# Decode attention on one core: TensorE's loop staggered by one head, K and V loads interleaved, the last head's first V half loaded into a K buffer

## The chip, the cores and the metric

The kernel runs on one core of a Trainium2 chip. The metric is the device time of one execution in microseconds (us). Before the change the median of 14 runs is 650.09 us, the lowest 648.61, the highest 654.18.

A core has engines that run side by side, each with its own instruction stream: PE (TensorE, matrix products), DVE (VectorE), ACT (ScalarE), POOL (GpSimd) and SP (SyncE, which issues loads here). They order themselves by semaphores. Data come from HBM by 16 transfer (DMA) engines, which work through the loads in the order in which SP issues them.

## The reference

```python
B, Hq, Hkv, Sq, Sk, D = 1, 32, 8, 1, 65536, 128     # bfloat16
k = jnp.repeat(k, 4, axis=1); v = jnp.repeat(v, 4, axis=1)
scores = jnp.einsum("bhqd,bhkd->bhqk", q, k) * D ** -0.5
p = softmax(scores)
out = jnp.einsum("bhqk,bhkd->bhqd", p, v)
```

One query row for each of 32 heads; four query heads share one of 8 K/V heads, each with 65,536 keys of 128 numbers. K and V together are 268.4 MB, which are read once; the output is 8 KB. "Head" below means one of the 8 K/V heads with its four queries.

## The kernel before

**Halves and slots.** A head's K, and its V, is loaded in two halves (`load`, L124), each 128 partitions x 256 keys x 128 numbers, 8.4 MB. The text writes K10 for head 1, half 0. The buffer `io` (L73) has three slots of one half each: slot 0 takes every V half, slot 1 the K halves 0, slot 2 the K halves 1. A load may be issued only when its slot has been used. SP issues all loads in one written order (L156 to 162): K00, K01, and then V00, K10, V01, K11, V10, K20 and so on. Ahead of each load SP waits for a count: for a K half that the scores from the slot's last content are done (`s_sc`, L130), for a V half that the slot's values are done (`s_vc`, L136). While SP waits, everything behind it in its order waits too. The last V half (L146 to 154) comes in six pieces, the first issued when the first half of the slot is free (`s_va`).

**A head on the engines.** DVE turns each K half in four quarters of 64 keys, in place (`transposes`, L214), and tells PE by `s_kt`. PE computes scores (L329 to 346): a loop of 8 steps, two steps to a bank of the PSUM tile `sc`, 16 matmuls to a step, 128 in all. The addresses of the matmuls are computed from the loop's counter in registers (`r_k`, `r_w`, `r_o`, L330 to 332). DVE takes the maximum of each bank (`bank_max`), the maxima go across the partitions by way of PE and DVE (`softmax`, L227; PE L347 to 353), and ACT computes the exponentials and their sums (L241). DVE turns the exponentials to weights for the values (`weights`, L249, one V half at a time into the tile `et`), and PE multiplies them with V (`wide`, L357): 64 matmuls for a half, which go in turn to four groups of PSUM rows of `vacc` (`32 * c`). For the last V half four of them are left out, and 16 small matmuls (L392 to 398) take their place, as soon as the last two pieces have landed. DVE adds up the four groups (`collect`, L260), PE adds across partitions (L389), DVE scales (`finish`, L273), and the result is stored.

**PE's order.** PE's program is a loop over the 8 heads (L320). In one turn: clear `sc` and `vacc` with five matmuls, all scores of head h, maximum and row sums of head h, values of head h from V half 0 and half 1, sum across partitions. So no score of head h + 1 is computed before the last value of head h. `take` (L306) is a wait on a semaphore that also takes the count off.

**Around it.** q is loaded four times into four groups of 32 partitions by ACT's queue (L165); DVE turns it (L178), and POOL copies each head's part into `wz` (L208), the moving window of score weights.

Of the kernel before, what the change touches and what calls it, by code (L numbers as in the profile page):

```python
# [21 lines left out]
TAIL = 16  # L22

# [23 lines left out]
def kernel(  # L47
# [29 lines left out]
    q_in = sb("q_in", [P, D], bf16)  # L77
# [23 lines left out]
    pl, fin = pf[0:H, 256:260], pf[0:H, 0:D]  # L101

    s_q, s_ka, s_kb, s_st = sem("s_q"), sem("s_ka"), sem("s_kb"), sem("s_st")
    s_v = [sem(f"s_v{i}") for i in range(4)]
    s_last = sem("s_last")
# [6 lines left out]
    s_sc, s_pe, s_va, s_vb, s_vc = sem("s_sc"), sem("s_pe"), sem("s_va"), sem("s_vb"), sem("s_vc")  # L112
# [16 lines left out]
    def load_k(g, b):  # L129
        SP.wait((s_sc, 8 * (g - 1) + 4 * b + 4 if g else 0))  # L130
        load(k, g, b, 1 + b, (s_ka, s_kb)[b])

    def load_v(g, b):
        n = 2 * g + b
        if g < G - 1:
            SP.wait((s_vc, n))  # L136
            load(v, g, b, 0, s_v[0])
            for s in s_v[1:]:
                sp.sem_inc(s, 16)
        elif b == 0:  # L140
            SP.wait((s_vc, n))
            load(v, g, b, 0, s_v[0], 0, 128)
            load(v, g, b, 0, s_v[1], 128, SL)
            for s in s_v[2:]:
                sp.sem_inc(s, 16)
        else:  # L146
            SP.wait((s_va, n))
            load(v, g, b, 0, s_v[0], 0, 128)
            SP.wait((s_vc, n))
            load(v, g, b, 0, s_v[1], 128, 192)  # L150
            load(v, g, b, 0, s_v[2], 192, 224)
            load(v, g, b, 0, s_v[3], 224, 240)
            load(v, g, b, 0, s_last, 240, 248)
            load(v, g, b, 0, s_last, 248, 256)
# [3 lines left out]
    for g in range(G):  # L158
        for b in range(2):
            load_v(g, b)  # L160
            if g < G - 1:
                load_k(g + 1, b)


    for a in range(4):  # L165
        act.dma_start(out=q_in[32 * a:32 * a + 32, :], in_=q[0, :, 0, :]).then_inc(s_q, 16)
# [10 lines left out]
    DV.wait((s_q, 64))  # L177
    d_qT = DV.mark(dve.transpose(  # L178
        out=qT[:, :, :].rearrange("p s n -> p (s n)"), in_=q_in[:, :].bitcast(u32)
    ))  # L180
# [9 lines left out]
    d_sel = DV.mark(dve.tensor_reduce(  # L190
        out=sely[:, :], in_=selq[:, :].rearrange("p (y h) -> p y h", h=H), axis=AX.X, op=ALU.add
    ))

# [5 lines left out]
    for g in range(G):  # L199
        if g == 0:  # L200
            GP.wait((s_dv, d_qT))
            GP.after(p_ident)
        else:
            GP.wait((s_sc, 8 * g))
        for a in range(4):
            r = slice(32 * a, 32 * a + 32)
            c0 = 28 + 32 * a
            gp.tensor_copy(  # L208
                out=wz[r, :, c0:c0 + H].rearrange("p (s w) h -> p s w h", s=2),
                in_=qTb[r, :, :, g, :],  # L210
            ).then_inc(s_w, 1)


    def transposes(g, b):  # L214
        DV.wait(((s_ka, s_kb)[b], 16 * (g + 1)))
        for t0 in range(0, SL, PS):
            part = io[:, (1 + b) * SL + t0:(1 + b) * SL + t0 + PS, :].rearrange("p t d -> p (t d)")
            dve.transpose(out=part.bitcast(u32), in_=part.bitcast(u32)).then_inc(s_kt, 1)  # L218
            yield

    def bank_max(g, b):
        DV.wait((s_sc, 8 * g + 2 * b + 2))
        return DV.mark(dve.tensor_reduce(  # L223
            out=mx[:, b:b + 1], in_=sc[:, 512 * b:512 * b + 512], axis=AX.X, op=ALU.max
        ))

    def softmax(g):  # L227
        dve.tensor_reduce(out=mg[:, :], in_=mx[:, :], axis=AX.X, op=ALU.max).then_inc(s_mg, 1)
        DV.wait((s_pe, 4 * g + 1))
        n = DV.mark(dve.tensor_reduce(  # L230
            out=m4[:, :], in_=pt[0:1, 0:P].rearrange("o (x h) -> o h x", h=H), axis=AX.X, op=ALU.max
        ))
        DV.after(n)
        dve.tensor_scalar_mul(
            out=nrow[:, :, :], in0=m4[:, None, :].to_broadcast([1, 32, H]), scalar1=-SCALE
        ).then_inc(s_nr, 1)
        DV.wait((s_pe, 4 * g + 2))
        d_nmb = DV.mark(dve.tensor_copy(out=nmb[:, :], in_=pb[:, 0:1]))  # L238
        ACTQ.wait((s_dv, d_nmb))
        for b in range(4):  # L240
            a = act.activation(  # L241
                out=ex[:, b, :], in_=sc[:, 512 * b:512 * b + 512], func=ACT.Exp, bias=nmb[:, :],
                scale=SCALE, accum_out=ls[:, b:b + 1],
            )
            ACTQ.mark(a)
        act.wait_ge(s_ac, ACTQ.n)
        act.sem_inc(s_ls, 1)
# [6 lines left out]
    def reciprocal(g):  # L254
        DV.wait((s_pe, 4 * g + 3))
# [25 lines left out]
    d_rl = None  # L281
    for g in range(G):
        for _ in transposes(g, 0):
            pass
        if g:
            DV.wait((s_vc, 2 * g))
            collect()
            finish(g - 1, 4 * g, d_rl)
        bank_max(g, 0)
        for i, _ in enumerate(transposes(g, 1)):  # L290
            if i == 1:
                bank_max(g, 1)
        bank_max(g, 2)
        DV.after(bank_max(g, 3))
        softmax(g)
        weights(g, 0)
        d_rl = reciprocal(g)
        DV.wait((s_vc, 2 * g + 1))
        weights(g, 1)
    DV.wait((s_vb, 2 * G))  # L300
    collect()
    finish(G - 1, 4 * G + 1, d_rl)
# [15 lines left out]
    pe.wait_ge(s_gp, p_ident)  # L318
    pe.wait_ge(s_dv, d_sel)
    with nc.Fori(0, G, 1, engines=OrderedEngineSet([PE]), head_slot={PE: 0}) as h:  # L320
# [7 lines left out]
        take(s_w, 4)  # L328
        with pe.Fori(0, 8) as p:  # L329
            r_k = pe.snap(p * (PS * D) + SL * D)  # L330
            r_w = pe.snap((p % 2) * (-16) + 28)
            r_o = pe.snap((p // 2) * 512)
            take(s_kt, 1)
            i = None
            for u in range(4):
                for s in range(2):
                    for e in range(2):
                        i = pe.matmul(  # L338
                            out=bass.AP(sc, r_o, [[2048, P], [1, 512]]),
                            lhsT=bass.AP(wz, r_w + ((2 * s + e) * WB - 4 * u), [[4 * WB, P], [1, P]]),  # L340
                            rhs=bass.AP(
                                io, r_k + (u * D + 64 * s + e), [[IO, P], [4 * D, 16], [2, 32]]
                            ),
                            start=False, stop=False, skip_group_check=True,
                        )
            i.then_inc(s_sc, 1)
        take(s_mg, 1)  # L347
        pe.transpose(out=pt[0:1, 0:P], in_=mg[:, :], identity=ident[:, :]).then_inc(s_pe, 1)  # L348
        take(s_nr, 1)
        pe.matmul(  # L350
            out=pb[:, 0:1], lhsT=nrow[:, :, :].rearrange("o x h -> o (x h)"), rhs=one[:, :],
            start=True, stop=True,
        ).then_inc(s_pe, 1)
        take(s_ls, 1)
        pe.matmul(out=pl, lhsT=sel[:, :], rhs=ls[:, :], start=True, stop=True).then_inc(s_pe, 1)  # L355

        def wide(ch, tt):  # L357
            c = tt % 4
            return pe.matmul(  # L359
                out=vacc[32 * c:32 * c + 16, :, :],  # L360
                lhsT=et[:, ch // 2, tt * 32 + 16 * (ch % 2):tt * 32 + 16 * (ch % 2) + 16],
                rhs=io[:, PS * ch + 4 * tt:PS * ch + 4 * tt + 4, :],
                start=False, stop=False, skip_group_check=True,
            )

        with pe.Fori(0, 2) as j:
            take(s_et, 2)
            take(s_v[0], 16)
            for tt in range(16):
                wide(0, tt)  # L370
            for tt in range(16):
                i = wide(1, tt)
            i.then_inc(s_va, 1)
            take(s_v[1], 16)
            for tt in range(16):
                wide(2, tt)
            take(s_v[2], 16)
            for tt in range(8):
                wide(3, tt)
            take(s_v[3], 16)  # L380
            for tt in range(8, 12):
                i = wide(3, tt)
            i.then_inc(s_vb, 1)
            with pe.If(h * 2 + j < 2 * G - 1):
                for tt in range(12, 16):
                    i = wide(3, tt)
                i.then_inc(s_vc, 1)
        take(s_vs, 1)
        pe.matmul(out=fin, lhsT=sel[:, :], rhs=vs[:, :], start=True, stop=False,  # L389
                  skip_group_check=True).then_inc(s_pe, 1)  # L390
    pe.wait_ge(s_last, 32)
    for x in range(TAIL):  # L392
        t = SL - TAIL + x
        o_ = (12 + x // 4) * 32 + 16 + 4 * (x % 4)
        i = pe.matmul(  # L395
            out=fin, lhsT=et[:, 1, o_:o_ + H], rhs=io[:, t, :], start=False,
            stop=(x == TAIL - 1), skip_group_check=True,
        )
    i.then_inc(s_pe, 1)
# [30 lines left out]
```

## Time and profile before

| | |
|---|---|
| median of 14 runs | 650.09 us |
| the profiled execution | 648.25 us |
| its span, first to last instruction | 646.3 us |
| mean granted PE clock | 0.804 |
| busy: PE, DVE, ACT, POOL | 347.5, 344.2, 23.5, 7.8 us |
| read from HBM | 268.47 MB, 415 GB/s over the span |
| K quarters turned by DVE (L218) | 64 x 4415 ns |
| score matmuls (L338) | 1024, 232.6 us busy |
| value matmuls (L359) | 1020, 92.2 us busy |

All durations come from one profiled execution. Its own time is 1.95 us more than its span, and it lies 1.84 us below the median. The page of the profile cuts the span in 40 slices of 16.2 us; a digit is the busy share in tenths. Groups of instructions are listed with their line, engine, what they write and read, their count, the busy time and the mean duration of one. PE's time has three parts: matmuls (PE), weight loads (PEld) and the sequencer (PEq or PEldq), which reads the program, computes addresses in registers, branches and waits; the sequencer's instructions are not counted as busy. A matmul's recorded duration (0.38 us for 512 columns at full clock) overlaps with its neighbours', so the pace is read from their starts. A number in brackets at the end of a line in order of time is how long the engine had been idle before it, and what ended that.

### The profile page before, as it was taken

To read this page: it belongs to the slowest core of one execution; us is meant where nothing else is said; L and a number is where in the kernel's file an instruction comes from. 1 tells how busy PE (TensorE), PEld (TensorE's weight loads), DVE (VectorE), ACT (ScalarE), POOL (GpSimd) and SP (SyncE) were. 2 spreads that over 40 slices of the span, in tenths; PEclk is the share of its full clock that TensorE was granted. 3 is DMA by queue.
4 is the path that set the end of the run, shared out by engine and by line. 5 is a ranking of instruction groups with operands and counts; after the bars stand their busy time and mean duration, and the time that the engine had idled before them with its cause. 6 is when DMAs were issued, how large, how long until landed. Compare 5 with 4: busy or idle time off the path is not lost. (4 is left out here: it accounts for less than half of the span.)

```text
span 646.3 us, 6464 instructions
## 1 busy us (share of the span) xinstructions
PE 347.5 (54%) x2156; PEld 141.9 (22%) x2156; DVE 344.2 (53%) x221; ACT 23.5 (4%) x65; POOL 7.8 (1%) x40
## 2 busy tenths in 40 slices
PE   0197405973079640876138760498406873088535
PEld 0033102431024210332013320143102331033212
DVE  0498282572917647194552927438292573917501
ACT  0000100001000100001000010000100001000100
POOL 1000000000000000000000000000000000000000
PEclk9999757996569965998759976589757997589975
DMA  9999999999999999999999999999999999999365
GB/s 391 452 393 450 450 398 442 442 414 439 434 426 442 438 418 442 438 418 446 430 426 446 438 414 446 434 418 450 430 422 446 426 434 438 426 435 416 152 286 233
DMA packets 5733, 268.53 MB, mean 416 GB/s; under 512 B 864, under 2 KB 864, under 8 KB 1248
## 3 DMA queue, kind: packets, MB, share of 16 engines
q1 hardware_dynamic: 5480, 268.44, 96.4%
q10 hardware_dynamic: 248, 0.04, 0.0%
q14 instruction: 4, 0.03, 0.0%
q8 instruction: 1, 0.02, 0.0%
HBM read 268.47 MB, written 0.01 MB: 415 GB/s over the span
## 5 line engine op out<-in xcount | busy, mean ns | idle before, releaser
L218 DVE STREAM_TRANSPOSE io<-io 128x4096 uint32<-128x4096 uint32 x64 | 279.5, 4415 | 36.2 <-DMA io<-in_k_dram 36.2
L338 PE MATMUL sc<-io,wz 128*128 x1024 | 232.6, 382 | 31.1 <-PEq L309 31.1
L359 PE MATMUL vacc<-io,et 128*16 128x512 bf16 x1020 | 92.2, 538 | 183.2 <-PEq L309 183.2
L338 PEld LDWEIGHTS sc<-io,wz 128*128 x1024 | 99.1, 97 | 164.6 <-issue 53.2
L359 PEld LDWEIGHTS vacc<-io,et 128*16 128x16 bf16 x1020 | 32.6, 117 | 239.7 <-issue 232.7
L223 DVE TENSOR_REDUCE mx<-sc 128x1 f32<-128x512 f32 x32 | 21.5, 670 | 88.8 <-PE sc L338 88.8
L252 DVE STREAM_TRANSPOSE et<-ex 128x512 bf16<-128x512 bf16 x32 | 21.5, 701 | 52.0 <-PE vacc L359 45.2
L241 ACT ACTIVATE ex<-sc,nmb 128x512 bf16<-128x512 f32 x32 | 21.5, 685 | 587.1 <-DVE nmb L238 587.1
L261 DVE TENSOR_SCALAR vs<-vacc,sely 128x128 f32<-128x128 f32 x8 | 2.8, 351 | 72.7 <-PE vacc L359 72.7
L324 PE MATMUL sc<-zero 128*128 128x512 bf16 x32 | 10.2, 450 | 27.9 <-DVE sely L190 27.1
L355 PE MATMUL pf<-ls,sel 128*4 128x4 f32 x16 | 1.5, 166 | 25.6 <-PEq L309 25.6
L178 DVE STREAM_TRANSPOSE qT<-q_in 128x64 uint32<-128x64 uint32 x1 | 0.2, 246 | 24.3 <-DMA q_in<-in_q_dram 24.3
L208 POOL COPY wz<-qT 32x16 bf16<-32x16 bf16 x32 | 6.1, 190 | 523.0 <-PE sc L338 498.6
L389 PE MATMUL pf<-vs,sel 128*4 128x128 f32 x16 | 3.2, 285 | 13.7 <-PEq L309 13.7
L324 PEld LDWEIGHTS sc<-zero 128*128 128x128 bf16 x32 | 2.8, 103 | 32.2 <-issue 30.7
L264 DVE SCALAR_TENSOR_TENSOR vs<-vacc,sely,vs 128x128 f32<-128x128 f32 x24 | 8.4, 351 | 0.9
L348 PE MATMUL pt<-ident,mg 128*1 128x128 f32 x8 | 2.2, 270 | 8.5 <-PEq L309 8.5
L355 PEld LDWEIGHTS pf<-ls,sel 128*4 128x4 f32 x16 | 0.9, 82 | 26.1 <-issue 26.1
L241 ACT ACTIVATION_READ_ACCUMULATOR ex<-sc,nmb 128x1 f32 x32 | 6.5, 203 | 0.0
L276 DVE TENSOR_SCALAR o<-pf,rl 4x128 bf16<-4x128 f32 x8 | 2.7, 339 | 6.8 <-PE pf L389 4.3
L350 PE MATMUL pb<-one,nrow 1*128 1x1 f32 x16 | 2.8, 241 | 5.7 <-PEq L309 5.7
L256 DVE TENSOR_REDUCE l<-pf 4x1 f32<-4x4 f32 x8 | 1.2, 150 | 8.1 <-PE pf L355 8.1
(25 smaller groups left out, 24.2 us busy)
## 6 DMA issues: line engine op xcount, KB each, us to landing
io<-in_v_dram SPq DMA_DIRECT2D x3, 4096.0 KB, 23.3
io<-in_v_dram SPq DMA_DIRECT2D x1, 2048.0 KB, 14.8
io<-in_v_dram SPq DMA_DIRECT2D x1, 1024.0 KB, 16.9
io<-in_v_dram SPq DMA_DIRECT2D x1, 512.0 KB, 17.7
io<-in_v_dram SPq DMA_DIRECT2D x2, 256.0 KB, 18.0
io<-in_k_dram SPq DMA_DIRECT2D x16, 38.8
io<-in_v_dram SPq DMA_DIRECT2D x14, 28.4
out_dram<-o ACTq DMA_DIRECT2D x7, 1.0 KB
```

Of the source, the lines that this page charges most:

```text
L208: gp.tensor_copy(out=wz[r, :, c0:c0 + H].rearrange("p (s w) h -> p s w h", s=2), in_=qTb[r, :, :, g, :],).then_inc(s_w, 1)
L218: dve.transpose(out=part.bitcast(u32), in_=part.bitcast(u32)).then_inc(s_kt, 1)
L223: return DV.mark(dve.tensor_reduce(out=mx[:, b:b + 1], in_=sc[:, 512 * b:512 * b + 512], axis=AX.X, op=ALU.max))
L241: a = act.activation(out=ex[:, b, :], in_=sc[:, 512 * b:512 * b + 512], func=ACT.Exp, bias=nmb[:, :], scale=SCALE, accum_out=ls[:, b:b + 1],)
L252: dve.transpose(out=et[:, i, :], in_=ex[:, 2 * b + i, :]).then_inc(s_et, 1)
L261: n = DV.mark(dve.tensor_scalar_mul(out=vs[:, :], in0=vacc[:, 0, :], scalar1=sely[:, 0:1]))
L264: i = dve.scalar_tensor_tensor(out=vs[:, :], in0=vacc[:, y, :], scalar=sely[:, y:y + 1], in1=vs[:, :], op0=ALU.mult, op1=ALU.add,)
L324: pe.matmul(out=bank, lhsT=zero[:, 0:P], rhs=zero[:, :], start=True, stop=False, skip_group_check=True,)
L338: i = pe.matmul(out=bass.AP(sc, r_o, [[2048, P], [1, 512]]), lhsT=bass.AP(wz, r_w + ((2 * s + e) * WB - 4 * u), [[4 * WB, P], [1, P]]), rh ...
L350: pe.matmul(out=pb[:, 0:1], lhsT=nrow[:, :, :].rearrange("o x h -> o (x h)"), rhs=one[:, :], start=True, stop=True,).then_inc(s_pe, 1)
L359: return pe.matmul(out=vacc[32 * c:32 * c + 16, :, :], lhsT=et[:, ch // 2, tt * 32 + 16 * (ch % 2):tt * 32 + 16 * (ch % 2) + 16], rhs=io[: ...
L389: pe.matmul(out=fin, lhsT=sel[:, :], rhs=vs[:, :], start=True, stop=False, skip_group_check=True).then_inc(s_pe, 1)
```

## The change

**Loads.** The order becomes K00, K01, V00, K10, K11, V01 and from there K20, V10, K21, V11, ..., K70, V60, K71, V61, V70, V71. K waits on the same condition (its counts are doubled, as a score step now has 8 matmuls); V waits for the values of the V half before it, as it did. V70, the first V half of the last head, goes to slot 1, a K slot, in two parts of 128 keys each, when the scores of K70 are done. V71 goes to slot 0 in six pieces, all issued when the values of V61 are done. q is loaded once, and DVE turns it four times.

**PE.** The loop has 9 turns. In turn h, for j = 0 and 1: scores of half j of head h (if h < 8), then values of half j of head h - 1 (if h > 0). Behind both come maximum and its broadcast for head h. The sum across partitions (`gather`) and the row sums of the head before stand at the beginning of a turn, ahead of the clearing; in the first turn they run on zeros that DVE has written. Score steps have 8 matmuls instead of 16, in a loop inside the loop over j, with both counters in the addresses. V70's values are 16 steps of 4 matmuls with addresses in registers, all into the rows 0 to 15 of `vacc`. The 16 small matmuls now come ahead of the last sum across partitions.

**DVE.** In turn g: turn K half 0 of head g; weights of half 1 of head g - 1; turn K half 1; maxima; reciprocal and `collect` of head g - 1; `softmax` and weights of half 0 of head g; `finish` of head g - 1.

The diff, cut to its core:

```diff
-pl, fin = pf[0:H, 256:260], pf[0:H, 0:D]
+pl, fin = pb[0:H, 8:12], pf[0:H, 0:D]
...
     def load_k(g, b):
-        SP.wait((s_sc, 8 * (g - 1) + 4 * b + 4 if g else 0))
+        SP.wait((s_sc, 16 * g - 8 + 8 * b if g else 0))
...
         elif b == 0:
-            SP.wait((s_vc, n))
-            load(v, g, b, 0, s_v[0], 0, 128)
-            load(v, g, b, 0, s_v[1], 128, SL)
...
+            SP.wait((s_sc, 16 * g + 8))
+            for i in range(2):
+                load(v, g, b, 1, s_u[i], 128 * i, 128 * i + 128)
         else:
-            SP.wait((s_va, n))
-            load(v, g, b, 0, s_v[0], 0, 128)
-            SP.wait((s_vc, n))
...
+            SP.wait((s_vc, 2 * g))
+            for lo, hi, s in zip(CUTS, CUTS[1:], s_v):
+                load(v, g, b, 0, s, lo, hi)
...
-    for g in range(G):
-        for b in range(2):
-            load_v(g, b)
-            if g < G - 1:
-                load_k(g + 1, b)
-    for a in range(4):
-        act.dma_start(out=q_in[32 * a:32 * a + 32, :], in_=q[0, :, 0, :]).then_inc(s_q, 16)
+    load_v(0, 0)
+    load_k(1, 0)
+    load_k(1, 1)
+    load_v(0, 1)
+    for g in range(2, G):
+        for b in range(2):
+            load_k(g, b)
+            load_v(g - 1, b)
+    load_v(G - 1, 0)
+    load_v(G - 1, 1)
+    act.dma_start(out=q_in[:, :], in_=q[0, :, 0, :]).then_inc(s_q, 16)
...
+    GP.wait((s_sc, 16 * G))
+    gp.sem_inc(s_w, 4)
+    for i in range(2):
+        GP.wait((s_u[i], 16))
+        gp.sem_inc(s_un, 128 // UN)
...
+    with nc.Fori(0, G + 1, 1, engines=OrderedEngineSet([PE]), head_slot={PE: 0}) as h:
+        take(s_w, 4)
+        take(s_vs, 1)
+        gather(start=True, stop=True).then_inc(s_pe, 1)
+        take(s_ls, 1)
+        pe.matmul(out=pl, lhsT=sel[:, :], rhs=ls[:, :], start=True, stop=True).then_inc(s_pe, 1)
...
+        with pe.Fori(0, 2) as j:
+            with pe.If(h < G):
+                with pe.Fori(0, 8) as n:
+                    r_k = j * (SL * D) + (n // 2) * (PS * D) + (n % 2) * (2 * D) + SL * D
+                    r_w = (n % 4) * (-8) + 28
+                    r_o = j * 1024 + (n // 4) * 512
+                    take(s_kt, 1)
+                    for u in range(2):
...
+                    i.then_inc(s_sc, 1)
+            with pe.If(h * 2 + j > 1):
+                take(s_et, 2)
+                with pe.If(h * 2 + j == 2 * G):
+                    with pe.Fori(0, SL // UN) as n:
+                        r_v = n * (UN * D) + SL * D
+                        r_e = (n // 8) * 512 + (n // 4) % 2 * 16 + (n % 4) * 128
+                        take(s_un, 1)
+                        for c in range(4):
+                            i = pe.matmul(
+                                out=vacc[0:16, :, :],
+                                lhsT=bass.AP(et, r_e + c * 32, [[1024, P], [1, 16]]),
+                                rhs=bass.AP(io, r_v + c * (4 * D), [[IO, P], [1, 4 * D]]),
+                                start=False, stop=False, skip_group_check=True,
+                            )
+                        i.then_inc(s_vu, 1)
+                with pe.Else():
...
+                    i.then_inc(s_vb, 1)
+                    with pe.If(h < G):
...
+                        i.then_inc(s_vc, 1)
+        with pe.If(h < G):
+            take(s_mg, 1)
...
     for x in range(TAIL):
...
+        if x % 8 == 0:
+            pe.wait_ge(s_v[len(CUTS) - 3 + x // 8], 16)
...
+    pe.wait_ge(s_vs, 1)
+    gather(start=False, stop=True).then_inc(s_pe, 1)
```

Here `UN` is 16, `SL` 256, `G` 8, and `CUTS` is 0, 128, 192, 224, 240, 248, 256.

## The prediction

> **What bounds the kernel now.** I read the 40 slices first, then the stretches at the end, then the order of time around the loads.
>
> ```profile
> DMA  9999999999999999999999999999999999999365
> GB/s 391 452 393 450 450 398 442 442 414 439 434 426 442 438 418 442 438 418 446 430 426 446 438 414 446 434 418 450 430 422 446 426 434 438 426 435 416 152 286 233
> ```
>
> The transfer engines are full in 37 of 40 slices; neither PE (54%) nor DVE (53%) is. So the time is 32 loads of 8.4 MB, plus the stretches in which no load may start. The next view gives stretches of 3 to 4 us; its last two columns are DMA share and GB/s, the one before is the granted PE clock.
>
> ```profile
> 600.00:604.00 4.00, 3.65 (x16) 1.53 (x16) 4.00 (x2) 0.00 (x0) 0.00 (x0) 1.00 0.82 352
> 604.00:608.00 4.00, 3.46 (x16) 1.54 (x16) 0.49 (x1) 0.00 (x0) 0.00 (x0) 1.00 0.00 0
> ...
> 612.00:616.00 4.00, 1.89 (x22) 0.75 (x26) 1.30 (x4) 1.60 (x6) 0.00 (x0) 0.50 0.00 0
> 616.00:619.00 3.00, 3.00 (x40) 1.16 (x36) 0.00 (x0) 0.00 (x0) 0.00 (x0) 0.59 0.23 66
> ```
>
> From about 604.8 to 618.9 nothing moves: 14.1 us. All of K is in, the one V slot still holds the first V half of head 7, and PE does not reach it until the softmax of head 7 is done. That is what the change goes for.
>
> The pace of the loads is read from DVE's waits for K, in order of time:
>
> ```profile
> 82.41 17.43 DVE L218 STREAM_TRANSPOSE io<-io 128x4096 uint32<-128x4096 uint32 x4 [3.31 <-DMA io<-in_k_dram]
> ...
> 585.89 8.77 DVE L218 STREAM_TRANSPOSE io<-io 128x4096 uint32<-128x4096 uint32 x2 [2.52 <-DMA io<-in_k_dram]
> ```
>
> K of head 1, half 0 (call it K10) is load 4, K71 is load 30: (585.89 - 82.41) / 26 = **19.37 us a load**. A load that finds the queue empty costs more:
>
> ```profile
> 617.93 4.40 SPq L125 DMA_DIRECT2D io<-in_v_dram  x6
> ...
> 630.07 3.59 PE L359 MATMUL vacc<-io,et 128*16 128x512 bf16 x32 [10.12 <-PEq L309]
> ```
>
> Half a load took 12.1 us from issue to use, 2.4 more than 19.37 / 2.
>
> **The change, part by part.**
>
> *Order of loads: the gap at 604.8 goes, another comes early.* The new order is K00 K01 V00 K10 K11 V01 K20 V10 K21 V11 and so on. V01 waits until PE has used V00, and PE now uses V00 only behind the scores of K10. V00 lands at 63, K10 at 82.4, K11 at 101.8; SP stands at V01's wait, with K20 and all later loads behind it. So the question is when the scores of K10 end. DVE needs 4.4 us for the first quarter, so PE starts at 86.8. PE's pace then comes from its sequencer. These are the sequencer's rows of one score step of 16 matmuls, and of the loop's edge before it (count, then ns min/median/max):
>
> ```profile
> L338 PEldq FUSED_REGOPS  x17: 74/74/110, 114.0 to 116.7; - x17
> ...
> L338 PEldq ALU_OP  x1: 36/36/36, 114.4 to 114.4; - x1
> ```
>
> ```profile
> L329 PEldq ALU_OP  x1: 32/32/32, 113.4 to 113.4; - x1
> L329 PEldq COMPARE_BRANCH  x1: 209/209/209, 113.5 to 113.5; - x1
> L329 PEldq MOVE  x1: 29/29/29, 113.8 to 113.8; - x1
> ```
>
> Every matmul with a register in its address has one fused register instruction, and in the trace their starts lie 0.153 us apart. The edge, from the ALU_OP at 113.40 to the first fused instruction at 114.05, is 0.64 us. The first matmul's addresses (two heavier fused instructions and one ALU_OP) take 0.45. So a step of 16 is 0.64 + 0.45 + 15 x 0.153 = 3.39 us, just under the 16 x 0.216 = 3.46 of its matmuls: today PE hides it. The change halves the step to 8 matmuls and puts two loop counters into the addresses: about 21 register operations instead of 13 for the first one, which I price at 0.66. A step is then 0.64 + 0.66 + 7 x 0.153 = **2.37 us against 1.73 of matmuls: the sequencer becomes the bound**. Eight steps are 19.0 us a half (14.1 now; DVE's four transposes take 17.4). From 86.8 the first step needs 1.9 without its edge, seven more 16.6, the last matmul 0.4, PE's cold start about 0.8: scores end at 106.4. Two branches and four takes of semaphores (1.3, partly beside the last matmuls), then 64 value matmuls, warm 3.4: V00 is used at 110.8. V01 is issued at 110.9 and lands 2.4 + 19.37 later, at 132.7, not at 121.1. **New gap: 11.6 us.** Bounds: 8.6 (steps hidden behind DVE: last quarter at 99.8, its scores 4.3, values 3.9, so 108.0 + 2.4 - 101.8) to 14 (a step of 2.7).
>
> *Steady state.* A V half is used 19.4 after its K half landed plus some 9, that is at L + 29, and the next load must be issued before L + 38.7 - 2.4: 7 us to spare. No further gap; DVE's moved pieces (collect, maxima, weights) are the same instructions and sit in that slack.
>
> *Start.* q as one load instead of four takes away DVE's wait until 25.4, but K10 needs its slot only at 63, so nothing is gained. Four small q transposes and two memsets lie before K00 lands. Sum of the start: 0. Moving the row sums to another bank, doubled counts, clearing before the first head and POOL's extra increments: 0, behind the same slack (without it, POOL passes V70's landing on with one more semaphore, 0.1 to 0.2 us, once).
>
> *Last head.* Loads run on without a gap: load 29 (K71) lands at 132.7 + 23 x 19.37 = 578.2, load 32 at 636.3. Scores of K71: quarters at 582.6, 587.0, and after two maxima of 0.65 at 592.7, 597.1; two steps each, end 602.4. Values of V61 until 606.9. Then collect (1.5), and from DVE's maximum of the transposed row to the row sums 4.4 us as in before (609.56 to 613.98): 612.8. Five clearing matmuls and the branches: PE starts on V70 at **615**.
>
> *V70 from the K buffer.* 16 steps of 4 matmuls, all with register addresses and into one group of 16 PSUM rows. The four column groups of the old form ran beside each other (next row: 20 weight loads in 0.96 us, 0.048 each); now each matmul has its full 0.216.
>
> ```profile
> 618.48 0.96 PEld L359 LDWEIGHTS vacc<-io,et 128*16 128x16 bf16 x20 [0.24 <-issue]
> ```
>
> By matmuls a step is 0.86 warm, 1.71 cold. By the sequencer: edge 0.64, first addresses (about 15 operations, four of them divisions or remainders) 0.53, three more at 0.153: **1.63**. 16 x 1.63 = 26.1 us: until 641.1. Bounds for the step: 0.86 (no register cost shows) and 1.9 (a fused instruction more for each matmul but one); I take 1.63, since the score loop is the same kind of code. Then two weight transposes, which wait for all of V70 (the buffer is the same), 1.5, and PE's takes and branches, 0.8: 643.6 allowing 0.2 to drain. V71, all landed by then, 60 packed matmuls, 3.3 warm to 5.7 cold: **648**.
>
> One rule speaks for a much better end. The Trainium skill, "TensorE: Matmul & The Clock Gate", Part 2, Back-to-back issue gap, gives N/2.4 + 2.5 ns for a warm matmul, 216 ns at N = 512; the trace agrees where nothing else binds (64 score matmuls in 14.10 us). By it alone V70 would cost 13.8 us. It does not count register addresses, and the rows above do. The same page, Part 1, lets the clock fall only after some 3.4 us of idling; so it would stay up in a loop that idles under 1 us a step. No row here shows a loop that sparse, and cold or warm differ by 1.71 - 1.63 a step, 1.3 us in all.
>
> *Tail.*
>
> ```profile
> 638.75 0.60 PE L359 MATMUL vacc<-io,et 128*16 128x512 bf16 x4 [0.27 <-PEq L309]
> 639.40 0.35 DVE L261 TENSOR_SCALAR vs<-vacc,sely 128x128 f32<-128x128 f32 x1 [18.09 <-PE vacc L359]
> ...
> 641.05 0.59 PE L389 MATMUL pf<-vs,sel 128*4 128x128 f32 x2 [1.71 <-PEq L309]
> 641.43 1.91 PE L395 MATMUL pf<-io,et 128*4 128x128 bf16 x16
> 643.44 0.34 DVE L276 TENSOR_SCALAR o<-pf,rl 4x128 bf16<-4x128 f32 x1 [2.54 <-PE pf L395]
> ```
>
> From the last wide matmul (639.35) to the end (646.3) it is 6.95 now. The 16 small matmuls move ahead of the sum over the groups and lie beside DVE's collect: 1.7 less, 5.3.
>
> **Sum.** 648 + 5.3 = 653.3 us of span, 7 more than 646.3: 14.1 of gap gone, 11.6 of new gap, and a PE end that follows the last load by 17 us instead of some 6 (transfers end shortly before 640 now). The profiled execution took 648.25, 1.95 over its span, and the median of 14 runs is 1.84 over that: 653.3 + 3.8 = **657**.
>
> **Rivals.**
> - *V70 fits behind the loads* (the other side). If V70's steps cost only their matmuls, ten cold at 0.427 and 54 at 0.216, it takes 15.9: 630.9, weights and takes 2.5, V71 3.3: 636.7, about when the last pieces land (636.3). Span 642.0, time **646**. It decides at a step of about 1.2 us (657 less 16 x 0.43 is the median of now): below that the change gains. For it: PE's busy time alone; against it: the 0.64 edge and 0.53 of addresses, which four matmuls can't cover. 20%.
> - *Between the two*: steps of 1.1 to 1.25, or 1.4 with the start gap of 8.6: within 0.2% of now, which is about what can be told from no change. 10%.
> - *Addresses do not fold*: each score matmul takes two fused instructions (0.28 a matmul). A step is 3.3, a half 26.5: the start gap grows by 7, V70's step to 2.0, together **670**. Against it: 17 fused instructions for 16 matmuls with two moving operands today. 8%.
> - Anything else, mostly slower (PE cold in every half): 2%.
>
> My forecast has 60%, between 652 and 663. Faster 0.20, same 0.10, slower 0.70. For the range: from the better rival with a last-load end slightly earlier (644) to the top of my own case (664).
>
> **What would show it.** Right: no DMA gap near 605 but one near 102 to 113; score halves of about 19 us; V70's steps 1.6 us apart with PE half idle; last bytes near 636 and an end near 653. Wrong: V70's steps near 0.9 us, or the start gap missing, or gaps in every head.

## The result, and the profile after

The changed kernel takes 656.11 us (median of 10 runs) against 650.07 for the kernel before in the same comparison: ratio 1.009, 95% interval 1.0067 to 1.0113. It is slower by 0.9%. The forecast was 657 us. The profiled execution took 656.02 us, its span is 653.9, 7.6 more than before.

The 40 slices of the page of the kernel after, transfer share and GB/s (a slice is now 16.3 us):

```profile
DMA  9999992999999999999999999999999999999980
GB/s 382 449 445 393 445 449 68 449 413 422 449 445 425 413 449 445 433 405 449 445 441 401 445 445 449 393 445 445 446 405 433 449 445 417 421 449 415 432 376 1
```

The hole in the third slice from the end is gone. But the seventh slice holds only 68 GB/s, and in the last one, 16 us long, next to nothing is loaded and the kernel still runs. In the trace transfers stand still from 101.3 to 112.4, 11.1 us, where the 14.1 us near 605 were before. The last piece lands at 638.6, 1.3 us earlier than in the kernel before (639.9). So most of the 14.1 us was given back at the start (11.1), 1.8 more went to two loads that took longer, and the loss itself lies behind the last landing: 15.3 us from there to the end, 6.4 before.

The stretches of the start gap, with the granted clock, the transfer share and GB/s in the last three columns:

```profile
96.00:101.00 5.00, 3.89 (x18) 1.53 (x16) 3.91 (x1) 0.00 (x0) 0.00 (x0) 1.00 0.52 223
101.00:106.00 5.00, 3.79 (x17) 1.48 (x16) 0.00 (x0) 0.00 (x0) 0.00 (x0) 1.00 0.00 0
106.00:112.00 6.00, 5.17 (x72) 2.16 (x70) 0.51 (x1) 0.00 (x0) 0.00 (x0) 1.00 0.00 0
```

In it PE works through the scores of K10, alone: DVE's last quarter ended at 99.9. PE in order of time:

```profile
100.60 1.92 PE L370 MATMUL sc<-io,wz 128*128 x8 [0.64 <-DVE io L227]
103.11 1.91 PE L370 MATMUL sc<-io,wz 128*128 x8 [0.60 <-issue]
105.63 1.91 PE L370 MATMUL sc<-io,wz 128*128 x8 [0.61 <-issue]
107.81 3.63 PE L339 MATMUL vacc<-io,et 128*16 128x512 bf16 x64 [0.27 <-PEq L325]
111.48 0.33 SPq L128 DMA_DIRECT2D io<-in_v_dram  x1
```

A step of 8 matmuls starts every 2.52 us and is busy for 1.9 of them. In the last two steps the idle 0.6 is put down to "issue": the profile shows nothing that PE waited for. The sequencer's row for these matmuls, in a window of one step:

```profile
L370 PEldq FUSED_REGOPS  x12: 47/74/226, 101.6 to 104.1; - x12
```

Between the edge of the loop and the next matmul it works on the first addresses, with single instructions of up to 226 ns. Then come the values of V00, and at 111.48 SP may issue V01 (the last line above).

The end of the kernel after, PE's and DVE's lines:

```profile
640.91 1.02 PE L390 MATMUL vacc<-io,et 128*16 x4 [0.68 <-PEq L325]
642.64 1.02 PE L390 MATMUL vacc<-io,et 128*16 x4 [0.70 <-PEq L325]
643.70 1.30 DVE L263 STREAM_TRANSPOSE et<-ex 128x512 bf16<-128x512 bf16 x2 [29.29 <-PE vacc L390]
...
645.56 3.41 PE L339 MATMUL vacc<-io,et 128*16 128x512 bf16 x60 [1.90 <-PEq L325]
648.80 1.06 PE L423 MATMUL pf<-io,et 128*4 128x128 bf16 x16
...
651.07 0.34 DVE L287 TENSOR_SCALAR o<-pf,rl 4x128 bf16<-4x128 f32 x1 [0.53 <-PE pf L335]
```

V70's loop runs from 617.3 to 643.7, a step every 1.71 us. The sequencer's rows of one of its steps, from the answer for that line in a window of one step:

```profile
L390 PEldq FUSED_REGOPS  x6: 42/74/247, 623.2 to 624.1; - x6
L390 PEld LDWEIGHTS vacc<-io,et x4: 85/85/86, 623.8 to 624.3; 128*16 x4
```

Six register instructions for four matmuls, one of them of 247 ns. A low clock is not what makes the step 1.71 us long, although four matmuls at 0.427 would add up to just that; the granted clock (third column from the end) is 1.00 in the loop:

```profile
620.00:632.00 12.00, 7.18 (x28) 2.39 (x28) 0.00 (x0) 0.00 (x0) 0.00 (x0) 1.00 0.97 416
```

Everything of V71 is there by 638.6, and PE comes to it at 645.6.

### The profile page after: what moved, and what is told of

The parts are those of the page before. It is cut to its first block, busy times and chain, and to the rows that moved or that the text cites. A ratio compares the mean times of both kernels' runs of the same rounds, so it can differ in the third digit from the quotient of the medians.

```text
span 653.9 us, 7257 instructions
## 1 busy us (share of the span) xinstructions
PE 375.9 (57%) x2167; PEld 147.6 (23%) x2167; DVE 342.4 (52%) x226; ACT 23.6 (4%) x65; POOL 7.9 (1%) x40
## 5 line engine op out<-in xcount | busy, mean ns | idle before, releaser
L370 PE MATMUL sc<-io,wz 128*128 x1024 | 273.1, 419 | 216.5 <-PEq L325 174.7
L370 PEld LDWEIGHTS sc<-io,wz 128*128 x1024 | 106.3, 104 | 386.6 <-issue 308.8
L339 PE MATMUL vacc<-io,et 128*16 128x512 bf16 x956 | 54.2, 379 | 5.2 <-PEq L325 5.2
L339 PEld LDWEIGHTS vacc<-io,et 128*16 128x16 bf16 x956 | 24.3, 89 | 35.0 <-issue 12.2
L390 PE MATMUL vacc<-io,et 128*16 x64 | 16.9, 391 | 9.4 <-PEq L325 8.9
L356 PE MATMUL sc<-zero 128*128 128x512 bf16 x36 | 17.0, 627 | 0.0
L352 PE MATMUL pb<-ls,sel 128*4 128x4 f32 x18 | 1.8, 169 | 18.7 <-PEq L325 18.7
L390 PEld LDWEIGHTS vacc<-io,et 128*16 x64 | 5.5, 87 | 21.2 <-issue 17.7
L414 PEld LDWEIGHTS pb<-one,nrow 1*128 1x128 f32 x16 | 2.3, 182 | 15.6 <-issue 15.6
L356 PE MATMUL vacc<-zero 128*128 128x512 bf16 x9 | 5.7, 634 | 0.0
```

The source lines that it names most:

```text
L339: return pe.matmul(out=vacc[32 * c:32 * c + 16, :, :], lhsT=et[:, ch // 2, w0:w0 + 16], rhs=io[:, PS * ch + 4 * tt:PS * ch + 4 * tt + 4, : ...
L356: pe.matmul(out=bank, lhsT=zero[:, 0:P], rhs=zero[:, :], start=True, stop=False, skip_group_check=True,)
L370: i = pe.matmul(out=bass.AP(sc, r_o, [[2048, P], [1, 512]]), lhsT=bass.AP(wz, r_w + ((2 * s + e) * WB - 4 * u), [[4 * WB, P], [1, P]]), rh ...
L390: i = pe.matmul(out=vacc[0:16, :, :], lhsT=bass.AP(et, r_e + c * 32, [[1024, P], [1, 16]]), rhs=bass.AP(io, r_v + c * (4 * D), [[IO, P], [ ...
L414: pe.matmul(out=pb[:, 0:1], lhsT=nrow[:, :, :].rearrange("o x h -> o (x h)"), rhs=one[:, :], start=True, stop=True,).then_inc(s_pe, 1)
```

## The experiments

**My theory** has two terms. First, PE's sequencer is the bound in both register loops; this makes the scores of a half end 25 us after its K has landed, and with V00 used only behind K10's scores it makes the start gap. Second, V70's register loop keeps PE 26 us on that half, so that the end follows the last landing by 15 us. **Rivals:** V70 is slow because its matmuls all go to one group of PSUM rows and no longer run beside each other; the scores are paced by DVE or by the matmuls; the start gap is made good later. Each experiment is timed in three rounds against the kernel before.

**V70 with fixed addresses.** The loop is written out; the rows stay the same.

```diff
-                    with pe.Fori(0, SL // UN) as n:
-                        r_v = n * (UN * D) + SL * D
...
+                    for n in range(SL // UN):
+                        take(s_un, 1)
...
+                                lhsT=et[:, w0 // 512, w0 % 512:w0 % 512 + 16],
+                                rhs=io[:, SL + n * UN + 4 * c:SL + n * UN + 4 * c + 4, :],
```

> The changed kernel with V70's 64 matmuls written out with fixed addresses (no loop, no registers), still all into rows 0 to 15. Register theory (the sequencer's address work makes a step of four 1.71 us): V70 takes about 14.5 us instead of 26.3 (ten cold matmuls at 0.43, 54 at 0.216), ends near 632, V71 is then held by its own last pieces (637.3), span near 643, about 11 less, time near 645. Ungrouped theory (V70 is slow because its matmuls no longer run beside each other in four row groups, the registers cost nothing): V70 stays at 26 us, span stays at 654.

Measured: 644.81 us, ratio to the kernel before 0.9919 (0.9894 to 0.9943), span 642.6. PE from V70 on:

```profile
617.05 14.90 PE L389 MATMUL vacc<-io,et 128*16 128x512 bf16 x64
633.85 3.20 PE L339 MATMUL vacc<-io,et 128*16 128x512 bf16 x56 [1.91 <-PEq L325]
637.28 0.39 PE L339 MATMUL vacc<-io,et 128*16 128x512 bf16 x4 [0.23 <-PEq L325]
638.31 1.05 PE L422 MATMUL pf<-io,et 128*4 128x128 bf16 x16 [0.64 <-DMA io<-in_v_dram]
```

The same 64 matmuls into the same rows take 14.9 us instead of 26.3, and now PE waits for V71's last pieces. So 11.4 us of V70's time were addresses and the loop. The ungrouped theory, by which V70 stays at 26 us, is out, and this edit alone makes the change a gain. (Ten cold matmuls and 54 warm ones, as in the expectation, add up to 16.0 us and not 14.5; in the trace about five ran cold, and five cold and 59 warm ones are 14.9.)

**V70 in 8 steps of 8.** `UN` is 32 and the loop over `c` has 8 turns.

```diff
-                        r_e = (n // 8) * 512 + (n // 4) % 2 * 16 + (n % 4) * 128
+                        r_e = (n // 4) * 512 + (n // 2) % 2 * 16 + (n % 2) * 256
...
-                        for c in range(4):
+                        for c in range(8):
```

> The changed kernel with V70 in 8 steps of 8 matmuls instead of 16 of 4, still by registers and into rows 0 to 15. Register theory: a step is 1.71 + 4 x 0.152 = 2.32 us, V70 takes about 18.5 us instead of 26.3, span near 646, time near 648. Ungrouped theory: the number of matmuls is the same, so V70 and the span stay.

Measured: 647.26 us, ratio 0.9958 (0.9943 to 0.9972), span 645.2. Two steps:

```profile
628.39 1.89 PE L390 MATMUL vacc<-io,et 128*16 x8 [0.44 <-issue]
630.74 1.89 PE L390 MATMUL vacc<-io,et 128*16 x8 [0.47 <-issue]
```

A step is 2.34 us (2.32 expected), 1.17 for four matmuls, V70 takes 17.9 us. The price sits in the edge and the first addresses of a step; half as many of them save 8.4 us.

**Fixed addresses, four groups of rows again.** The kernel with V70's fixed addresses, its matmuls going in turn to the four groups; the diff is against that kernel.

```diff
-                                out=vacc[0:16, :, :],
+                                out=vacc[32 * c:32 * c + 16, :, :],
```

> As the kernel with fixed addresses for V70, and the matmuls go in turn to four groups of PSUM rows again. Theory now (with fixed addresses the end hangs on V71's last pieces, not on V70): V70 falls from 14.9 to 4 to 6 us, PE then waits for V71's first pieces, span stays within 0.7 us of that kernel's 642.6. Ungrouped theory: the matmuls' own time is the cost, span falls by several us more.

Measured: 645.56 us, ratio 0.9925 (0.9897 to 0.9953), span 643.3.

```profile
616.80 5.17 PE L389 MATMUL vacc<-io,et 128*16 128x512 bf16 x64
628.41 3.59 PE L339 MATMUL vacc<-io,et 128*16 128x512 bf16 x32 [6.45 <-PEq L325]
...
637.04 0.61 PE L339 MATMUL vacc<-io,et 128*16 128x512 bf16 x4 [0.21 <-PEq L325]
638.07 1.59 PEld L422 LDWEIGHTS pf<-io,et 128*4 128x4 bf16 x16 [0.93 <-DMA io<-in_v_dram]
638.08 1.87 PE L422 MATMUL pf<-io,et 128*4 128x128 bf16 x16 [0.43 <-issue]
```

V70 falls from 14.9 to 5.2 us and the span gains nothing: PE idles 6.5 us ahead of V71. So running beside each other is worth 9.7 us of PE time and, once the addresses are fixed, none on the path. The end now hangs on the last landing.

**Score steps of 16.** The step is as long as in the kernel before.

```diff
-                with pe.Fori(0, 8) as n:
-                    r_k = j * (SL * D) + (n // 2) * (PS * D) + (n % 2) * (2 * D) + SL * D
...
-                    take(s_kt, 1)
-                    for u in range(2):
+                with pe.Fori(0, 4) as n:
+                    r_k = j * (SL * D) + n * (PS * D) + SL * D
...
+                    take(s_kt, 2)
+                    for u in range(4):
...
-                    i.then_inc(s_sc, 1)
+                    i.then_inc(s_sc, 2)
```

> The changed kernel with score steps of 16 matmuls instead of 8, as in the kernel before; V70 untouched. Register theory: a step is 2.52 + 8 x 0.152 = 3.74 us, under DVE's 4.4 for a quarter, so a half's scores end about 21.5 us after its K has landed instead of 25; the start gap shrinks from 11.1 to about 7.5 and K71's scores end 3 earlier: span 6 to 7 less, near 647. Rival (DVE's transposes or the matmuls set the pace of the scores): gap and span stay within 1.5 us.

Measured: 651.31 us, ratio 1.0019 (1.0001 to 1.0038), span 648.5.

```profile
87.71 16.82 PE L370 MATMUL sc<-io,wz 128*128 x64 [12.83 <-PEq L325]
108.14 0.33 SPq L128 DMA_DIRECT2D io<-in_v_dram  x1
```

The start gap is 7.9 us instead of 11.1, the scores of K10 end at 104.5 instead of 107.5, V01 is issued at 108.1 instead of 111.5, and V70 begins 5.4 us earlier. That is the span's gain, a little less than the 6 to 7 expected. So the sequencer paced the scores with steps of 8. With steps of 16 it is DVE's quarters again: the wait ahead of K10's last step ends at 99.9, when DVE has turned the last quarter.

**V00 loaded behind K10.** Only the order of two loads is exchanged.

```diff
-    load_v(0, 0)
     load_k(1, 0)
+    load_v(0, 0)
     load_k(1, 1)
```

> The changed kernel with V00 loaded behind K10 instead of ahead of it; nothing else. Start-gap theory: V00 is used soon after it has landed, the gap near 101 to 112 shrinks from 11.1 us to 2 or 3, every later load and V70 move up by 8 to 9, span near 645, time near 647. Rival (the start gap is made good later, and the end is set by PE's work on the last head alone): the gap shrinks, the span stays within 2 us of 654.

Measured: 652.01 us, ratio 1.0032 (1.0018 to 1.0046), span 650.3. Half a miss: the gap near 101 is gone, but I had left out that K10 now stands at the head of the queue when K01 has landed, and K10 waits for the scores of K00:

```profile
43.00:46.00 3.00, 2.40 (x11) 0.96 (x10) 2.10 (x1) 0.00 (x0) 0.00 (x0) 1.00 0.00 0
46.00:50.00 4.00, 2.95 (x13) 1.06 (x11) 4.00 (x2) 0.00 (x0) 0.00 (x0) 1.00 0.00 0
```

Transfers stand still from 43.5 to 50.6, 7.1 us. 11.1 less 7.1 is 4.0, the span fell by 3.6. That the gap is made good later is out as well: what the start gained, the end gained.

**Order, score steps of 16 and fixed addresses together.** No other edit.

> Fixed addresses in four groups for V70, score steps of 16, and V00 behind K10. Theory: the gap at the start is now the wait of K10 for K00's scores, 22.1 us after K00's landing (24.2) plus 2.4 of an empty queue, less 43.6: about 5 us instead of 11.1, and no second one; last landing near 632.6, span 4.2 behind it, near 637, time near 639. Rival (each loss hides another, gains do not add): span stays near the best so far, 642.

Measured: 638.71 us, ratio 0.9811 (0.9772 to 0.985), span 636.4. One gap of 4.0 us is left: the last bytes of K01 move at 43.1, and the first of K10, issued at 46.1, at 47.1 (I had said 5). A window inside it:

```profile
44.00:46.00 2.00, 2.00 (x10) 0.77 (x8) 2.00 (x1) 0.00 (x0) 0.00 (x0) 1.00 0.00 0
```

One by one the three edits shortened the span by 10.6, 5.4 and 3.6 us, 19.6 in all; together they shorten it by 17.5. So the gains nearly add.

**The same with K00 in four quarters**, so that PE's first scores begin when a quarter of K00 has landed (9.5 instead of 24).

```diff
-    load_k(0, 0)
+    for i in range(4):
+        load(k, 0, 0, 1, s_k0[i], PS * i, PS * i + PS)
...
```

> The kernel before in this list, and K00 loaded in four quarters, so that DVE and PE begin after the first. Theory: K00's scores end near 33, well ahead of 43.6; no gap over 1 us is left at the start; last landing near 627.5, span near 632, time near 634, faster than both kernels. Rival (a gap shows up elsewhere, as it did when only the order was changed): span at 636 or more.

Measured: 632.37 us, ratio **0.9713** (0.9675 to 0.9752), span 630.2: 2.9% faster than the kernel before, 24 us faster than the changed one. Its slices:

```profile
DMA  8999999999999999999999999999999999999995
GB/s 363 437 459 408 458 408 446 420 445 420 453 412 458 408 458 416 449 428 437 428 437 433 437 437 428 437 433 437 425 441 424 441 424 441 424 441 424 420 419 230
```

There is no gap from the first load to the last landing at 625.0.

**That kernel with V70 in the change's register loop again.**

> The kernel before in this list with V70 back in its register loop of 16 steps, as in the change. Theory (start gap and V70's loop add up, each by its own): span 654 less 11.1 (gap) less 3 (K71's scores), near 640, time near 642; V70 still takes 26 us and ends 12 us after its last landing. Rival (the loop is hidden once loads come earlier, or the start gap was not on the path): span equal to that of fixed addresses, or to 648.5 of the score steps alone.

Measured: 641.13 us, ratio 0.985 (0.981 to 0.9889), span 637.9.

```profile
626.60 1.02 PE L395 MATMUL vacc<-io,et 128*16 x4 [0.70 <-PEq L330]
629.53 3.42 PE L344 MATMUL vacc<-io,et 128*16 128x512 bf16 x60 [1.91 <-PEq L330]
```

The loop takes 26.3 us as before. It costs 7.7 us of span here; in the change it costs 10.6 (653.9 against 643.3 with fixed addresses in four groups). Most of the difference is that V70 begins 23.7 us ahead of the last landing instead of 21.3. So the loop is not hidden, and start and end add up. The program ends 12.9 us after the last landing; the expectation said 12 of V70 itself, which ends 2.6 us after it. The loads ran 2.5 us earlier than worked out (625.0 against 627.5), and the end came 2 earlier.

**The fastest kernel with V70 in the V slot**, as in the kernel before.

```diff
-            SP.wait((s_sc, 16 * g + 8))
-            for i in range(2):
-                load(v, g, b, 1, s_u[i], 128 * i, 128 * i + 128)
+            SP.wait((s_vc, 2 * g))
+            load(v, g, b, 0, s_v[0])
...
-            SP.wait((s_vc, 2 * g))
+            SP.wait((s_vc, 2 * g + 1))
...
```

> The fastest kernel so far (span 630.2) with V70 back in the V slot, as in the kernel before: V70 waits until V61 is used, V71 until V70 is used; everything else stays. Theory (the K slot for V70 is the part of the change that gains): V61 lands at 586.0 and is used at 593.4, so a gap of 9.8 ahead of V70; V70 lands near 615, is used near 619, a gap of 6 to 7 ahead of V71; last landing near 641.5, span near 646.5, 16 more. Rival (the staggered loop and the interleaved order alone had already closed the gap at the end): span stays within 3 us of 630.

Measured: 650.91 us, ratio 0.9995 (0.9973 to 1.0017), span 648.0. Two gaps, 8.8 us (585.4 to 594.2) and 7.0 us (614.8 to 621.8), and 17.8 us more of span. A window in each:

```profile
586.00:590.00 4.00, 3.98 (x24) 1.75 (x28) 0.29 (x1) 0.00 (x0) 0.00 (x0) 1.00 0.00 0
616.00:620.00 4.00, 4.00 (x52) 1.54 (x48) 0.00 (x0) 0.00 (x0) 0.00 (x0) 0.61 0.00 0
```

So nothing is gained without loading V70 into a K slot. Without it the staggered loop and the interleaved order, even with start and score steps mended, stand where the kernel before stands.

## Why the prediction was right, step by step

The sign, the size and the mechanism held; some terms were off by 1 to 3 us in both directions. That the total came within 0.9 us is in part luck. The scores of K71 ended 3.0 us later than forecast and V70 2.6 later, but V71 and the tail took less than forecast, so the span is only 0.6 over. The 3.8 us added to the span for a median was 2.2.

- *Gap at 605 goes:* yes, 14.1 us.
- *New start gap:* yes. The 11.6 us were the delay of V01's landing (132.7 instead of 121.1); it landed at 133.4, so 12.3. Transfers stood still for 11.1. The score step was mis-sized, 2.37 against 2.52, all in the first addresses: 0.82 us instead of 0.66, with register instructions of 182 and 226 ns among them. V00 was used at 111.4 (110.8), as less time than allowed passed between scores and values.
- *Steady state without a gap:* yes. Two loads were 0.8 and 1.0 us longer than 19.4 in the trace, for a cause that stays open. Mainly they, and V01's landing at 133.4 instead of 132.7, put K71 at 580.2 instead of 578.2.
- *V70 begins:* 615 forecast, 617.3 measured, mostly those 2 us. *A step:* 1.63 forecast, 1.71 measured (first addresses 0.60 instead of 0.53). *V70 ends:* 641.1 and 643.7.
- *V71 ends:* 648 and 649.0. PE's clock stayed up, so it took 3.4 us, the lower end of my 3.3 to 5.7.
- *Tail:* 5.3 forecast, 4.9 measured.
- *The rival on the other side* is what the fixed addresses are: 646 was given for a V70 that costs only its matmuls, 644.8 was measured, with 14.9 us for V70 (15.9). Its turning point, about 1.2 us a step, held too: 1.17 for four matmuls in the steps of 8 is faster by 0.4%.
- *The issue gap:* the trace has 14.9 us for V70 with fixed addresses, the first matmuls at the low clock, and 26.3 with registers. In this loop the sequencer's rows decide and not the gap of the matmuls. The Trainium skill's issue gap ("TensorE: Matmul & The Clock Gate", Part 2, Back-to-back issue gap) makes an estimate of 13.8 us for V70.

What the runs leave open: whether PE could use V00 ahead of K10's scores, which would take away the start gap without another order of loads, was not tried. Nor was the K slot alone, without the staggered loop. In the kernel before, the scores of K70 end at 589.6:

```profile
575.51 14.10 PE L338 MATMUL sc<-io,wz 128*128 x64
```

So a K slot was free 15 us before the transfers ran dry at 604.8, and V71 might have gone there. What the staggered loop adds to the K slot is therefore not shown.

## What to carry to other kernels

When transfers are the bound, a change of order has to be followed load by load from the first: ask for each slot when its content is used and which loads can fill the time until then; a gap that is closed at the end can open at the start, and mending that one can open a third. Price a short register loop on TensorE by its sequencer (edge, first addresses, then each matmul), not by its matmuls: steps of 4 and 8 matmuls were bound by it, one of 16 was not. And a kernel that is slower may hold a part that gains: here the K slot for V70 was worth 17.8 us of span in the staggered kernel with the two losses beside it removed.

## What the hardware showed that I had not expected

- A fused register instruction mostly takes 74 ns, but up to 257 ns among the first addresses of a step (the row of V70's step above shows one of 247). These addresses hold the divisions and remainders of the loop's counter. That they are the cause is likely, but the trace does not name what an instruction computes.
- PE's clock stays at its full value at a busy share of 60%. A later window of V70's loop in the kernel after:

```profile
632.00:644.00 12.00, 7.17 (x28) 2.39 (x28) 0.30 (x1) 0.00 (x0) 0.00 (x0) 1.00 0.36 141
```

PE is busy 7.17 of 12 us at a granted clock of 1.00. No pause here is longer than 0.7 us. With V70 in four groups PE idled for 6.5 us ahead of V71, and behind that the granted clock is 0.50 (628.4 to 632). The Trainium skill ("TensorE: Matmul & The Clock Gate", Part 1) lets the clock fall after some 3.4 us of idling. Both rows agree with it.
- A faster PE can make the end longer: with V70 in four groups PE waits for V71, and the 16 small matmuls at the very end take 1.87 us at a granted clock of 0.50 (638 to 640). Where V70 kept PE busy until shortly before, they take 1.05 us at 1.00. The span with four groups is 0.7 us longer, but by their ratios (0.9925 and 0.9919) the two kernels cannot be told apart.
